# Weight tails as one DMA each, a buffer for every pair's exponentials, and a new order of all steps in a linear-attention and Mish block

## The chip, the cores and the metric

The kernel runs on one core of a Trainium2 chip. A core has five engines that run side by side and meet through semaphores: TensorE (PE in the profile; PEld is its weight load), VectorE (DVE), ScalarE (ACT), GpSimd (POOL) and SyncE (SP), which here only issues DMAs. The core's 16 DMA engines carry the transfers. The metric is the device time of one execution in microseconds (us); the profile gives one execution with the start and duration of each instruction, and of each DMA packet.

## What is computed

x has 2048 rows of 448 columns. All is bfloat16. Cut to what matters:

```python
xn = (x - mean(x)) / sqrt(var(x) + 1e-5)
q, k, v = split_heads(xn @ wqkv)                  # 16 heads of 28
pq, pk = q @ w_phi[h], k @ w_phi[h]               # per head, 28 x 28
phi_q = concat(softmax(pq), softmax(-pq)); phi_k likewise
kv, z = phi_k^T v, sum over rows of phi_k         # per head
attn = (phi_q kv) / (phi_q z + 1e-6) @ wo
h = xn @ w1 + b1                                  # 448 -> 1792
ffn = (h * tanh(softplus(h))) @ w2                # Mish
out = x + attn + ffn
```

## The kernel before

The 2048 rows are 16 tiles t of 128, handled as eight pairs u. The 448 columns of a contraction are three chunks of 128 and a tail of 64. The two tiles of a pair keep their tails in the lower and the upper 64 partitions of one chunk, so that two products of 64 rows can run together on PE; the last 64 rows of each weight are for that reason loaded into both halves of the partitions (`load_tail`, L260 to L263, two DMAs of 64 rows each).

The program records every instruction in the order in which the steps of the string `ORDER` (L149 to L162) are called, one stream for each engine; `Program.resolve` (L91) then finds the semaphore waits from what each instruction reads and writes. So `ORDER`, written out, sets the order on every engine and on both DMA queues (SP's, and ACT's for the steps with the ending `a`). Each engine works strictly in its order: an instruction that waits holds all behind it. The steps:

- `lx0`, `lx1`, `lx2`, `lx4` load x (tiles 0-1, 2-3, 4-7, 8-15); `lqm` and `lqt`, `lkm` and `lkt`, `lvm` and `lvt`, `l1m` and `l1t` load the main part and the tail of the weights for queries, keys, values and W1; `lp` loads w_phi, `lb` b1, `l2` W2, `lo` Wo.
- `st`, `xn`: LayerNorm statistics of a pair (DVE, with two small ACT operations for the root) and the normalized rows (on DVE with the ending `d`, on POOL with `p`), in `NXN` buffers in turn. `xt`: transpose of a pair, by PE and a copy (`a`, `d`), or by a DMA transpose on SP (`m`).
- `wt`, `wm`: the weights for queries and keys are multiplied by w_phi on the chip. `w_tr` (L459) transposes them, eight 128-column pieces a half, `w_mm` (L474) multiplies by the block-diagonal `Wbd` into `Wpq` and `Wpk`.
- `v`, `k`, `q`, `f`: products of a pair, a group of 1024 rows q0 or q1, and of FFN1 column block fc. Each has a full part `F` (three chunks) and a half part `H` (the tail), both through `pair_part` (L364). Its two PSUM banks come from `take2` (L337), the pair of eight banks that has been untouched longest. The closing part calls the evacuation: a copy for values, exponentials on ACT for keys and queries, Mish on ACT for FFN1.
- `kn`: sums and reciprocals of a pair's exponentials (DVE) and their product (POOL, `phik`, L532). `kv`: 32 small products into one PSUM pair held from the first kv to `kvz`, which masks it into `KVZ`. `nd`: numerator and denominator of a tile and seven DVE operations. `ot`: DMA transpose of the result; `wo`, `g`: output projection and FFN2 into the same banks; `sto`, `stt`: stores.

Keys' exponentials, normalized keys and values have three buffers each, in turn over the eight pairs. Twelve products of zeros (`warm`) run on PE at the start.

Of the kernel before, what the change touches and what calls it, by code (L numbers as in the profile page):

```python
# [169 lines left out]
def _kernel(es, nc, A_x, A_wqkv, A_w_phi, A_wo, B_w1, B_b1, B_w2, out):  # L170
# [120 lines left out]
    op("POOL", lambda e: e.memset(ident[:], 0.0), w=[("ident",)])  # L291
    op("POOL", lambda e: e.memset(eps_col[:], float(LN_EPS)), w=[("eps",)])
    op("POOL", lambda e: e.affine_select(out=ident[:], in_=ident[:], compare_op=ALU.not_equal, fill=1.0,
                                         base=0, pattern=[[-1, P]], channel_multiplier=1),
       r=[("ident",)], w=[("ident",)])
    op("POOL", lambda e: e.memset(mask[:], 1.0), w=[("mask",)])
    op("POOL", lambda e: e.affine_select(out=mask[:], in_=mask[:], compare_op=ALU.is_ge, fill=0.0, base=0,
                                         channel_multiplier=1, pattern=[[-DH, 4]]),
       r=[("mask",)], w=[("mask",)])
    op("POOL", lambda e: e.affine_select(out=mask[:], in_=mask[:], compare_op=ALU.is_ge, fill=0.0, base=DH - 1,  # L300
                                         channel_multiplier=-1, pattern=[[DH, 4]]),
       r=[("mask",)], w=[("mask",)])
    for i in range(NPH):
        op("POOL", lambda e, i=i: e.memset(v_ext[i][:, :, :, DH:DH + 1], 1.0), w=[("v1", i)])
    op("POOL", lambda e: e.memset(Wbd[:], 0.0), w=[("Wbd0",)])

    op("POOL", lambda e: e.memset(mask2[:], 1.0), w=[("mask2",)])
    for r in range(2):
        lo, hi = HALF[r]
        op("POOL", lambda e, lo=lo, hi=hi: e.affine_select(  # L310
            out=mask2[lo:hi], in_=mask2[lo:hi], compare_op=ALU.is_ge, fill=0.0, base=0, channel_multiplier=1,
            pattern=[[-DH, 2]]), r=[("mask2",)], w=[("mask2",)])
        op("POOL", lambda e, lo=lo, hi=hi: e.affine_select(
            out=mask2[lo:hi], in_=mask2[lo:hi], compare_op=ALU.is_ge, fill=0.0, base=DH - 1, channel_multiplier=-1,
            pattern=[[DH, 2]]), r=[("mask2",)], w=[("mask2",)])
    op("POOL", lambda e: e.tensor_copy(ap_on(KVZ[:, 0, 0, 0, DH + 1:DH + 2], [[NDW, 2 * G], [DH + 2, 2]]),
                                       ap_on(mask2[:, 0:1], [[0, 2 * G], [1, 2]])), r=[("mask2",)], w=[("KVZ1",)])

    def warm(e):
        for n in range(NWARM):  # L320
            ins = e.matmul(bank(0)[:, :], zeros[:, 0:P], zeros[:, :], start=True, stop=True)
        return ins
    op("DVE", lambda e: e.memset(zeros.bitcast(mybir.dt.uint32), 0), w=[("zeros",)], tag="zeros")
    op("PE", warm, r=[("zeros",)], w=[pb(0)], tag="warm")


# [497 lines left out]
```

## Time and profile before

| what | us |
|---|---|
| median of three runs (161.26 to 162.41) | 161.29 |
| the profiled execution: its span | 160.7 |
| PE, first product of values begins (L376) | 14.18 |
| last PE products, begin 144.57 and 13.40 long: end | 157.97 |
| last store issued | 158.67 |
| POOL, last phik begins | 53.2 |
| DVE, first nd operation | 59.02 |

The span is the profiled execution's own time from its first to its last instruction; it was taken apart from the three timed runs. The page's second part cuts it into 40 slices of 4.0 us, a digit for each engine's busy share in tenths. A timeline line has start, busy time, engine, line, operation, output and inputs, sizes and count; in brackets is the idle time before it and what ended it. A DMA line has tensor, queue, number of issues, KB of each and the median time from issue to landing.

### The profile page before, as it was taken

Reading aid. Unit: us, or ns where it says so; the run is one execution under the profiler, and the core shown is the slowest. Engines: PE = TensorE matmul, PEld = TensorE weight load, DVE = VectorE, ACT = ScalarE, POOL = GpSimd, SP = SyncE. Lnnn points to the kernel's source line nnn. Section 1 sums busy time; section 2 is a strip of 40 time slices with the busy share of each in tenths; the row PEclk is TensorE's granted clock in tenths of the full one; section 3 lists DMA queues with packets and bytes.
Section 4 is the critical chain, followed back from the end, with each engine's and each line's share of the span. In section 5 each row is a group of like instructions: output and inputs, shape, how many; then the busy total and the mean of one; then the engine's idle time right before and its main releaser. Section 6 shows DMA issues by size and latency. Waiting matters only on the chain.

```text
span 160.7 us, 3100 instructions
## 1 busy us (share of the span) xinstructions
PE 152.4 (95%) x1300; PEld 74.5 (46%) x1300; DVE 100.9 (63%) x209; ACT 75.6 (47%) x91; POOL 45.5 (28%) x73
## 2 busy tenths in 40 slices
PE   6659999998999999999999999999999999999993
PEld 2346545453444544434444454454545554555551
DVE  1768799999968168910778589988928811311131
ACT  2355988895939949997668756300100000000000
POOL 6766699959989600000000000000000000000000
PEclk9996999999999999999999999999999999999999
DMA  5998948240498000200030203060070130000502
GB/s 146 284 354 129 183 76 324 40 81 2 70 329 259 8 0 4 57 0 0 4 57 0 57 4 57 0 61 0 2 168 8 23 91 0 0 33 0 225 4 86
DMA packets 21306, 12.96 MB, mean 81 GB/s; under 512 B 14892, under 2 KB 20524, under 8 KB 21292
## 3 DMA queue, kind: packets, MB, share of 16 engines
q1 hardware_dynamic: 20524, 12.39, 30.6%
q10 hardware_dynamic: 768, 0.37, 0.9%
q8 instruction: 10, 0.16, 0.4%
q14 instruction: 4, 0.03, 0.1%
HBM read 7.48 MB, written 1.84 MB: 58 GB/s over the span
## 4 chain that ended last, share of the span: by engine, by line
PE 82%; POOL 5%; DVE 5%; DMA 4%; SPq 2%; issue 1%
PE PS L376 41%; PE PS L692 27%; PE PS L707 7%; POOL phik L532 4%; DMA Wq<-in_A_wqkv_dram 4%; PE PS L623 3%; DVE xn L421 2%; PE PS L553 2%; PE PS L481 1%; DVE Sk L528 1%; POOL xn L416 1%; PE PS L468 1%; SPq L262 1%; DVE v_ext L435 1%; SPq L257 0%
## 5 line engine op out<-in xcount | busy, mean ns | idle before, releaser
L376 PE MATMUL PS<-xnT,W 128*128 128x512 bf16 (+1 forms) x224 | 45.9, 379 | 0.0
L692 PE MATMUL PS<-W,actT 128*128 128x448 bf16 x224 | 43.5, 353 | 0.0
L602 ACT ACTIVATE actT<-PS,b1T 128x1024 bf16<-128x1024 f32 x28 | 30.0, 1112 | 21.3 <-PE PS L376 21.3
L692 PEld LDWEIGHTS PS<-W,actT 128*128 128x128 bf16 x224 | 21.8, 98 | 20.9 <-issue 0.8
L376 PEld LDWEIGHTS PS<-xnT,W 128*128 128x128 bf16 (+1 forms) x224 | 17.5, 97 | 23.4 <-issue 4.9
L532 POOL TENSOR_TENSOR phik<-Ek,rSk 128x896 bf16<-128x896 bf16 x16 | 26.8, 1699 | 2.6 <-DVE rSk L530 2.5
L682 DVE TENSOR_TENSOR x_all<-PS,x_all 128x448 bf16<-128x448 f32 x16 | 9.8, 622 | 25.8 <-PE PS L692 24.6
L528 DVE TENSOR_REDUCE Sk<-Ek 128x32 f32<-128x896 bf16 x16 | 16.8, 1050 | 0.6 <-ACT Ek L518 0.6
L588 ACT ACTIVATE EqT<-PS 128x1024 bf16<-128x1024 f32 x16 | 15.2, 1030 | 0.4 <-PE PS L376 0.2
L518 ACT ACTIVATE Ek<-PS 128x896 bf16<-128x896 f32 x16 | 13.8, 915 | 3.3 <-PE PS L376 3.2
L376 PE MATMUL PS<-xnT,Wpq 128*128 128x512 bf16 (+1 forms) x64 | 13.9, 379 | 0.7 <-DVE v_ext L435 0.7
L639 DVE COPY Sq<-PS 128x16 f32<-128x16 f32 x32 | 4.0, 168 | 16.7 <-PE PS L623 16.5
L376 PE MATMUL PS<-Wpk,xnT 128*128 128x448 bf16 (+1 forms) x64 | 13.0, 356 | 0.0
L376 PE MATMUL PS<-Wv,xnT 128*128 128x448 bf16 (+1 forms) x64 | 12.9, 360 | 0.0
L416 POOL TENSOR_SCALAR xn<-x_all,rstd,shift 128x448 bf16<-128x448 bf16 (+2 forms) x21 | 12.1, 589 | 0.7
L395 DVE BATCH_NORM_STATS2 stats<-x_all 128x6 f32<-128x448 bf16 x16 | 9.5, 596 | 3.3 <-DMA x_all<-in_A_x_dram 3.3
L647 DVE TENSOR_TENSOR Ek<-Ek,phik 128x464 f32<-128x464 f32 x16 | 10.3, 642 | 0.6
L643 DVE TENSOR_TENSOR Ek<-PS,Sq 128x464 f32<-128x464 f32 x16 | 10.3, 642 | 0.5
L650 DVE TENSOR_TENSOR xn<-Ek,rden 128x448 bf16<-128x448 f32 x16 | 10.0, 625 | 0.6
L645 DVE TENSOR_TENSOR phik<-PS,Sq 128x464 f32<-128x464 f32 x16 | 10.1, 631 | 0.0
L376 PEld LDWEIGHTS PS<-xnT,Wpq 128*128 128x128 bf16 (+1 forms) x64 | 5.2, 97 | 7.0 <-DVE v_ext L435 1.1
L376 PEld LDWEIGHTS PS<-Wpk,xnT 128*128 128x128 bf16 (+1 forms) x64 | 5.1, 97 | 6.3 <-issue 2.1
...
## 6 DMA issues: line engine op xcount, KB each, us to landing
...
out_dram<-x_all SPq DMA_DIRECT2D x7, 224.0 KB, 2.1
W<-in_B_w_dram SPq DMA_DIRECT2D x1, 1344.0 KB, 6.2
...
Wo<-in_A_wo_dram SPq DMA_DIRECT2D x2, 336.0 KB, 9.3
...
W<-in_B_w_dram SPq DMA_DIRECT2D x2, 224.0 KB, 4.1
Wk<-in_A_wqkv_dram SPq DMA_DIRECT2D x1, 336.0 KB, 4.4
```

Of the source, the lines that this page charges most:

```text
L376: ins = e.matmul(o, lhs(c, k), rhs(c, k), start=first and c in (0, 3), stop=not first and c in (2, 3))
L416: op("POOL", lambda e, t=t, lo=lo, hi=hi, at=at: e.tensor_scalar(X[:, at:at + hi - lo], x_all[:, t, lo:hi], rstd[:, t:t + 1], shift[:, t:t ...
L518: op("ACT", lambda e, s=s: e.activation(Ek[i][:, s, :, :], two(b, D), ACT.Exp, scale=1.0 if s == 0 else -1.0), r=[pb(b), pb(b + 1)], w=[(" ...
L528: op("DVE", lambda e: e.tensor_reduce(Sk[i][:, s, :], Eh(), AX.X, ALU.add), r=[("Ek", i, s)], w=[("Sk", i, s)], tag=f"Sk{u}.{s}")
L532: op("POOL", lambda e: e.tensor_tensor(phik[j][:, s, :, :].rearrange("p i (h f) -> p (i h) f", f=DH), Eh(), ap_on(rSk[i][:, s, 0:1], [[1, ...
L588: op("ACT", lambda e, s=s: e.activation(EqT[:, s, g, q * 1024:(q + 1) * 1024], bank(b, 2), ACT.Exp, scale=1.0 if s == 0 else -1.0), r=[pb( ...
L602: op("ACT", lambda e: e.activation(actT[:, fc, q * 1024:(q + 1) * 1024], bank(b, 2), ACT.Mish, bias=b1T[:, fc:fc + 1]), r=[("b1T",), pb(b) ...
L643: op("DVE", lambda e: e.tensor_tensor(tv(t1[i]), num(0), sx(1), ALU.mult), r=[pb(b), pb(b + 1), ("Sq", i, 1)], w=[("t1", i)], tag=f"ta{t}")
L645: op("DVE", lambda e: e.tensor_tensor(tv(t2), num(1), sx(0), ALU.mult), r=[pb(b), pb(b + 1), ("Sq", i, 0)], w=[("t2",)], tag=f"tb{t}")
L647: op("DVE", lambda e: e.tensor_tensor(t1[i], t1[i], t2, ALU.add), r=[("t1", i), ("t2",)], w=[("t1", i)], tag=f"tc{t}")
L692: ins = e.matmul(bank(b)[:, 0:D], actT[:, fc, tok(t)], W2[:, fc, :], start=first and fc == 0, stop=last and fc == FC - 1)
L707: ins = e.matmul(bank(b)[:, 0:D], oT_of(u)[lo:hi, cc * P:(cc + 1) * P], Wo[lo:hi, cc, :], start=first and c in (0, 3), stop=last and c in ...
```

## The change

- Each tail is one DMA into all 128 partitions, whose source goes over the 64 rows twice by an outer step of zero. Keys' and values' weights lie in one tensor `Wkv` and share one tail of 64 rows by 896 columns. All loads are on SP's queue, in the order x1, x0, Wk, key/value tail, w_phi, b1, Wv, x2, x4, query tail, Wq; then transposes of pairs 2, 7, 6, 3, Wo, pair 4, W1 tail, pair 5, W1, W2.
- All eight pairs have their own exponentials, in columns of `actT` that FFN1 (blocks 6 to 13) fills later; they are normalized in place. Values of all pairs lie in one tensor, sums have eight buffers, xn four, and `WT` one per weight and half.
- The root of LayerNorm is a step of its own (`rs`), for seven pairs on POOL as an addition and a power of -0.5. Seven of eight pairs are normalized on DVE (one before); x1 and x0 are transposed on PE, the other six by DMA (one and seven before).
- The setup instructions of POOL, DVE and PE are steps of the order too. Values come ahead of keys, the pairs in the order 0, 1, 2, 7, 6, 3, 4, 5, and all kv steps after them, among the first FFN1 steps.

The diff, cut; what is left out is the setup as functions with the same instructions, and renamed operands.

```diff
--- before.py
+++ after.py
...
@@ -147,18 +146,18 @@
 
 
 ORDER = """
-lx1s lpa lx0a lqta lkts bd lkms lbs lx2s table st1 st0 b1 wtk1d wtk0a lqms xn1p lvts lvms wmk1a xn0p st2 lx4s
-wtq1d xt1d xn2p wmk0a wmq1a st3 wtq0d v1Hd k1H k1F xt0m st4 v1Fd wmq0a xn3p xn4p xt2m k0F v0Ha l1ts k0H k2H
-kn1.0 st7 xt3m kn1.1 v0Fa v2Fa v2Ha kn0.1 q0.2H k2F q0.2F kn0.0 xt4m v4Fd st5 xn5p k3F kn2.1 kv1 v4Hd k3H k4F
-kv0 k4H kn2.0 xn7d q0.0H q0.1H q0.1F kn3.0 l1ms xt5m q0.0F kn4.1 v3Fd k5F st6 kv2 v3Hd v5Ha xn6p k5H kn4.0 v5Fa
-q0.3F xt7m k7H xt6m q0.3H k7F v7Fd kv4 kn3.1 kv3 kn5.1 v6Ha kn5.0 v7Hd v6Fa k6F k6H q1.0H kn7.0 q1.2H kn7.1
-q1.0F q1.2F f1.3F l2s kn6.1 f0.7F f1.3H f0.7H kv5 kn6.0 kv7 kv6 f0.1F kvz f0.3F nd2 f1.2H f0.3H f0.1H f1.2F
-q1.1F nd3 q1.1H nd1 los q1.3H q1.3F f0.4H f0.4F f0.8F f0.2F f0.5F f0.8H f0.2H f0.5H f1.1H f1.1F f1.4F f0.0F
-f1.4H ot1m f0.0H f1.13H nd0 f1.13F f1.5F f1.7F f1.7H f1.6H nd7 f1.6F f1.10F ot0m f1.10H nd6 ot3m f1.5H f0.10H
-f0.10F f1.0F nd5 f1.0H f0.6H f0.11H f0.6F f0.11F f1.12F nd4 f1.11H f1.12H nd10 f1.11F f0.13F f0.12F f0.12H ot2m
-f0.13H nd8 f0.9H f0.9F f1.8F nd11 nd9 f1.8H wo0H g1 g0 wo0F ot5m wo3F nd14 wo3H nd15 ot7m f1.9H f1.9F g6 g7 g11
-ot4m wo5H wo2H nd12 nd13 wo5F g5 wo4F wo2F sto3 g10 ot6m g4 g15 wo7H wo6H wo1H sto0 wo4H g8 wo7F wo6F g13 wo1F
-stt15 g9 sto4 g12 g2 sto5 sto6 g3 sto2 sto1 g14 stt14
+pm table lx1s zero pk st1 lx0s lkms pv pw lkts pi lps rs1p z12 st0 lbs xn1d rs0a bd xn0d lvms wtk0a wtk1d lx2s b1
+xt1a xt0d wmk0a st2 wmk1a v0Fd rs2p lx4s v1Fa xn2d lqts k0H st7 v1Ha k1H v0Ha lqms xt2m k0F rs7p xn7d st6 k1F rs6p
+wtq0d wtq1d v2Hd k2H k2F v2Fa xt7m xn6d st3 wmq1a k7F rs3p wmq0a v7Fd v7Ha k7H xt6m k6H xn3d v6Ha xt3m kn2.0 st5 rs5p
+k6F st4 rs4p v6Fd xn4p los xn5d xt4m l1ts q0.2F kn6.0 k3H q0.2H xt5m q0.0H v3Hd kn0.0 k3F kn1.1 l1ms kn0.1 q0.0F
+q0.3F kn2.1 v3Fa k4F q0.3H k4H q0.1H kn7.0 v4Hd v4Fd q0.1F kn3.0 k5F v5Fd v5Hd l2s k5H q1.0H q1.3H kn5.0 q1.3F kn4.0
+kn7.1 kn6.1 q1.0F q1.2F kn3.1 f1.1F q1.2H f1.4H f1.1H f1.4F kn5.1 f0.1F kv7 kv2 kv6 kv0 f0.1H f0.3H q1.1H q1.1F f0.0F
+f0.3F kn4.1 kn1.0 kv4 kv1 kv3 kv5 f0.5F kvz f0.0H f0.8H f0.5H nd1 f0.8F f1.11F f0.4F f1.11H nd2 f0.4H f0.6F f0.6H nd3
+f0.11H f0.9H f0.11F f0.9F f0.10F f1.2H f0.10H ot1m nd0 f0.13H f1.2F f1.9F f0.13F f1.7F f1.7H nd6 f1.9H ot0m f1.12H
+f1.12F f0.12F nd4 f0.12H f1.6H nd5 f1.6F f0.2H f0.2F f0.7F ot2m f0.7H f1.3H nd7 f1.8H ot3m f1.8F f1.3F f1.0F f1.10F
+nd8 f1.10H f1.5H f1.0H f1.5F g1 wo0H nd10 f1.13H nd9 f1.13F g0 wo0F wo1F g3 ot4m nd12 nd13 wo1H wo3H g6 ot6m wo3F
+wo4F g7 g2 g9 nd11 sto1 ot5m wo4H nd15 nd14 g8 wo6F g12 g5 wo5F sto0 g13 ot7m g11 wo7F wo6H sto4 sto6 wo5H wo2H wo7H
+sto3 g14 g10 wo2F g4 g15 sto5 sto2 stt14 stt15
 """
 
...
+    eps_col = sb("eps_col", [P, 1], FP32)
+    mhalf = sb("mhalf", [P, 2], FP32)
...
-    NXN = 3
+    NXN = 4
...
-    Wv = sb("Wv", [P, 4, D], BF16)
-    Wqk = [sb("Wq", [P, 4, D], BF16), sb("Wk", [P, 4, D], BF16)]
+    Wkv = sb("Wkv", [P, 4, 2 * D], BF16)
+    Wk, Wv = Wkv[:, :, 0:D], Wkv[:, :, D:2 * D]
+    Wq = sb("Wq", [P, 4, D], BF16)
+    Wqk = [Wq, Wk]
...
-    WT = [sb(f"WT{i}", [GP, 2, G, P], BF16) for i in range(2)]
+    WT = [[sb(f"WT{w}{i}", [GP, 2, G, P], BF16) for i in range(2)] for w in range(2)]
...
-    NE = 3
-    Ek = [sb(f"Ek{i}", [P, 2, 2, D], BF16) for i in range(NE)]
-    Sk = [sb(f"Sk{i}", [P, 2, 2 * H], FP32) for i in range(NE)]
-    rSk = [sb(f"rSk{i}", [P, 2, 2 * H], FP32) for i in range(NE)]
-    NPH = 3
-    phik = [sb(f"phik{i}", [P, 2, 2, D], BF16) for i in range(NPH)]
-    v_ext = [sb(f"v_ext{i}", [P, 2, H, DH + 1], BF16) for i in range(NPH)]
+    Sk = [sb(f"Sk{i}", [P, 2, 2 * H], FP32) for i in range(NU)]
+    rSk = [sb(f"rSk{i}", [P, 2, 2 * H], FP32) for i in range(NU)]
+    v_flat = sb("v_all", [P, NU * 2 * H * (DH + 1)], BF16)
+    v_all = v_flat[:, :].rearrange("p (u i h c) -> p u i h c", u=NU, i=2, h=H)
...
+    def as_t(n):
+        return v_flat[:, :].bitcast(FP32)[:, n * H * (DH + 1):(n + 1) * H * (DH + 1)].rearrange("p (h c) -> p h c", c=DH + 1)
+
+    t1, t2 = [as_t(0), as_t(1)], as_t(2)
+
+    FE = FC - NU
+
+    def E_of(u):
+        return actT[:, FE + u, 0:4 * D].rearrange("p (s i d) -> p s i d", s=2, i=2)
+
+    oT_home = [(Wkv, 0, ["Wk", "Wv"]), (Wkv, 14 * P, []), (Wq, 0, ["Wq"]), (Wp[1], 0, ["Wp1"])]
+    home_rows = {"Wk": [("Wk", 0), ("Wt",)], "Wv": [("Wv", 0)], "Wq": [("Wq", i) for i in range(2)],
+                 "Wp1": [("Wp", 1, h) for h in range(2)]}
...
     def load_tail(eng, name, dst, src):
-        for i, (lo, hi) in enumerate(HALF):
-            dma(eng, lambda e, lo=lo, hi=hi: e.dma_start(dst[lo:hi, 3, :], src[384:448, :]), w=[(name, 1 + i)],
-                tag="ld" + name)
+        dma(eng, lambda e: e.dma_start(dst[:, 3, :], bass.AP(
+            tensor=src.tensor, offset=src[384:448, :].offset, ap=[[0, 2]] + [list(d) for d in src[384:448, :].ap])),
+            w=[("Wt",) if name == "Wkv" else (name, 1)], tag="ld" + name)
 
     def rows_of(name):
-        return [(name, i) for i in range(3)]
+        return [(name, 0), ("Wt",)] if name in ("Wk", "Wv") else [(name, i) for i in range(2)]
...
+    def p_ident():
+        op("POOL", lambda e: e.memset(mhalf[:], -0.5), w=[("mhalf",)], tag="mhalf")
+        op("POOL", lambda e: e.memset(eps_col[:], float(LN_EPS)), r=[("mhalf",)], w=[("eps",)], tag="eps")
+        op("POOL", lambda e: e.memset(ident[:], 0.0), w=[("ident",)], tag="pi0")
...
+    def ln_rstd(u, eng):
         a, b = 2 * u, 2 * u + 2
+        if eng == "POOL":
+            op("POOL", lambda e: e.tensor_scalar(lnv[:, a:b], mv[:, a:b, 1], float(LN_EPS), 0.0, op0=ALU.add,
+                                                 op1=ALU.add),
+               r=[("mv", a), ("mv", a + 1)], w=[("lnv", u)], tag=f"vare{u}")
+            op("POOL", lambda e: e.tensor_tensor(rstd[:, a:b], lnv[:, a:b], mhalf[:], ALU.pow),
+               r=[("lnv", u), ("eps",)], w=[("rstd", u)], tag=f"rstd{u}")
+            return
         op("ACT", lambda e: e.activation(lnv[:, a:b], mv[:, a:b, 1], ACT.Ln, bias=eps_col[:]),
            r=[("eps",), ("table",), ("mv", a), ("mv", a + 1)], w=[("lnv", u)], tag=f"ln{u}")
...
         if eng == "POOL":
-            op("POOL", lambda e: e.tensor_tensor(shift[:, a:b], mv[:, a:b, 0], rstd[:, a:b], ALU.mult),
+            op("DVE", lambda e: e.scalar_tensor_tensor(shift[:, a:b], mv[:, a:b, 0], -1.0, rstd[:, a:b], ALU.mult,
+                                                       ALU.mult),
                r=[("mv", a), ("mv", a + 1), ("rstd", u)], w=[("sh", u)], tag=f"sh{u}")
-            op("POOL", lambda e: e.tensor_scalar(shift[:, a:b], shift[:, a:b], -1.0, 0.0, op0=ALU.mult, op1=ALU.add),
-               r=[("sh", u)], w=[("sh", u)], tag=f"sj{u}")
...
-        pe(tr, rows_of("Wq" if which == 0 else "Wk") + [("ident",)], [pb(b)], f"wtr{which}{h}")
-        evac(eng, lambda: WT[h][:, :, :, :].rearrange("p c g n -> p (c g n)"),
-             lambda: oT().rearrange("p c g n -> p (c g n)"), [pb(b)], [("WT", h)], f"wtre{which}{h}")
+        pe(tr, rows_of("Wq" if which == 0 else "Wk")[:1 + 2 * h] + [("ident",)], [pb(b)], f"wtr{which}{h}")
+        evac(eng, lambda: WT[which][h][:, :, :, :].rearrange("p c g n -> p (c g n)"),
+             lambda: oT().rearrange("p c g n -> p (c g n)"), [pb(b)], [("WT", which, h)], f"wtre{which}{h}")
...
     def k_mm(u, part):
-        i = u % NE
-
         def then(b):
             for s in range(2):
-                op("ACT", lambda e, s=s: e.activation(Ek[i][:, s, :, :], two(b, D), ACT.Exp,
+                op("ACT", lambda e, s=s: e.activation(E_of(u)[:, s, :, :], two(b, D), ACT.Exp,
                                                       scale=1.0 if s == 0 else -1.0),
-                   r=[pb(b), pb(b + 1)], w=[("Ek", i, s)], tag=f"exk{u}.{s}")
+                   r=[pb(b), pb(b + 1)], w=[("E", u, s)], tag=f"exk{u}.{s}")
         pair_part(f"k{u}", part, tok_works(u, Wp[1]), [("xnT", u)] + [("Wp", 1, h) for h in range(2)], then)
 
     def k_norm(u, s):
-        i, j = u % NE, u % NPH
-
         def Eh():
-            return Ek[i][:, s, :, :].rearrange("p i (h f) -> p (i h) f", f=DH)
-        op("DVE", lambda e: e.tensor_reduce(Sk[i][:, s, :], Eh(), AX.X, ALU.add), r=[("Ek", i, s)], w=[("Sk", i, s)],
+            return E_of(u)[:, s, :, :].rearrange("p i (h f) -> p (i h) f", f=DH)
+        op("DVE", lambda e: e.tensor_reduce(Sk[u][:, s, :], Eh(), AX.X, ALU.add), r=[("E", u, s)], w=[("Sk", u, s)],
            tag=f"Sk{u}.{s}")
-        op("DVE", lambda e: e.reciprocal(rSk[i][:, s, :], Sk[i][:, s, :]), r=[("Sk", i, s)], w=[("rSk", i, s)],
+        op("DVE", lambda e: e.reciprocal(rSk[u][:, s, :], Sk[u][:, s, :]), r=[("Sk", u, s)], w=[("rSk", u, s)],
            tag=f"rSk{u}.{s}")
-        op("POOL", lambda e: e.tensor_tensor(phik[j][:, s, :, :].rearrange("p i (h f) -> p (i h) f", f=DH), Eh(),
-                                             ap_on(rSk[i][:, s, 0:1], [[1, 2 * H], [0, DH]]), ALU.mult),
-           r=[("Ek", i, s), ("rSk", i, s)], w=[("phik", j, s)], tag=f"phik{u}.{s}")
+        op("POOL", lambda e: e.tensor_tensor(Eh(), Eh(), ap_on(rSk[u][:, s, 0:1], [[1, 2 * H], [0, DH]]), ALU.mult),
+           r=[("E", u, s), ("rSk", u, s)], w=[("E", u, s)], tag=f"phik{u}.{s}")
...
-        pe(f, [("phik", j, 0), ("phik", j, 1), ("v", j), ("v1", j)], [pb(kvb)], f"kv{u}")
+        pe(f, [("E", u, 0), ("E", u, 1), ("v", u), ("v1",)], [pb(kvb)], f"kv{u}")
...
-               r=[("b1T",), pb(b), pb(b + 1)], w=[("act", fc, q)], tag=f"mish{q}_{fc}")
+               r=[("b1T",), pb(b), pb(b + 1)],
+               w=[("act", fc, q)] + ([("E", fc - FE, s) for s in range(2)] if fc >= FE else []), tag=f"mish{q}_{fc}")
...
-        for i, n in enumerate("qkv"):
-            args = eng, "W" + n, (Wqk + [Wv])[i], A_wqkv[:, i * D:(i + 1) * D]
-            add(f"l{n}m{c}", load_main, *args)
-            add(f"l{n}t{c}", load_tail, *args)
+        for i, (n, t) in enumerate((("q", Wq), ("k", Wk), ("v", Wv))):
+            add(f"l{n}m{c}", load_main, eng, "W" + n, t, A_wqkv[:, i * D:(i + 1) * D])
+        add(f"lqt{c}", load_tail, eng, "Wq", Wq, A_wqkv[:, 0:D])
+        add(f"lkt{c}", load_tail, eng, "Wkv", Wkv, A_wqkv[:, D:3 * D])
         add(f"l1m{c}", load_main, eng, "W1", W1, B_w1)
         add(f"l1t{c}", load_tail, eng, "W1", W1, B_w1)
```

More of the change, by code (lines that the diff above doesn't have):

```diff
@@ L26 @@
 DEN_EPS = 1e-6
-NWARM = 12
 QP = 56
@@ L287, in table @@
            tag="table")
[L291 to L324, printed above, removed]
+    def p_ident():
+        op("POOL", lambda e: e.memset(mhalf[:], -0.5), w=[("mhalf",)], tag="mhalf")
+        op("POOL", lambda e: e.memset(eps_col[:], float(LN_EPS)), r=[("mhalf",)], w=[("eps",)], tag="eps")
+        op("POOL", lambda e: e.memset(ident[:], 0.0), w=[("ident",)], tag="pi0")
+        op("POOL", lambda e: e.affine_select(out=ident[:], in_=ident[:], compare_op=ALU.not_equal, fill=1.0,
+                                             base=0, pattern=[[-1, P]], channel_multiplier=1),
+           r=[("ident",)], w=[("ident",)], tag="pi1")
@@ new lines, in p_mask @@
+    def p_mask():
+        op("POOL", lambda e: e.memset(mask[:], 1.0), w=[("mask",)], tag="pm0")
+        op("POOL", lambda e: e.affine_select(out=mask[:], in_=mask[:], compare_op=ALU.is_ge, fill=0.0, base=0,
+                                             channel_multiplier=1, pattern=[[-DH, 4]]),
+           r=[("mask",)], w=[("mask",)], tag="pm1")
+        op("POOL", lambda e: e.affine_select(out=mask[:], in_=mask[:], compare_op=ALU.is_ge, fill=0.0, base=DH - 1,
+                                             channel_multiplier=-1, pattern=[[DH, 4]]),
+           r=[("mask",)], w=[("mask",)], tag="pm2")
@@ new lines, in p_wbd, with p_ones, p_mask2 @@
+    def p_wbd():
+        op("POOL", lambda e: e.memset(Wbd[:], 0.0), w=[("Wbd0",)], tag="pw0")
+    def p_ones():
+        op("POOL", lambda e: e.memset(v_all[:, :, :, :, DH:DH + 1], 1.0), w=[("v1",)], tag="pv0")
+    def p_mask2():
+        op("POOL", lambda e: e.memset(mask2[:], 1.0), w=[("mask2",)], tag="pk0")
+        for r in range(2):
+            lo, hi = HALF[r]
+            op("POOL", lambda e, lo=lo, hi=hi: e.affine_select(
+                out=mask2[lo:hi], in_=mask2[lo:hi], compare_op=ALU.is_ge, fill=0.0, base=0, channel_multiplier=1,
+                pattern=[[-DH, 2]]), r=[("mask2",)], w=[("mask2",)], tag="pk1")
+            op("POOL", lambda e, lo=lo, hi=hi: e.affine_select(
+                out=mask2[lo:hi], in_=mask2[lo:hi], compare_op=ALU.is_ge, fill=0.0, base=DH - 1, channel_multiplier=-1,
+                pattern=[[DH, 2]]), r=[("mask2",)], w=[("mask2",)], tag="pk2")
+        op("POOL", lambda e: e.tensor_copy(ap_on(KVZ[:, 0, 0, 0, DH + 1:DH + 2], [[NDW, 2 * G], [DH + 2, 2]]),
+                                           ap_on(mask2[:, 0:1], [[0, 2 * G], [1, 2]])), r=[("mask2",)], w=[("KVZ1",)],
+           tag="pk3")
@@ L328, in _kernel, with zero, warm, f @@
+    def zero():
+        op("DVE", lambda e: e.memset(zeros.bitcast(mybir.dt.uint32), 0), w=[("zeros",)], tag="zeros")
+    def warm(n):
+        b = take1()
+        def f(e):
+            for _ in range(n):
+                ins = e.matmul(bank(b)[:, :], zeros[:, 0:P], zeros[:, :], start=True, stop=True)
+            return ins
+        pe(f, [("zeros",)], [pb(b)], f"warm{n}")
     clock = [0]
@@ L725, in _kernel @@
         add(f"st{u}", ln_stats, u)
+        for eng, c in (("ACT", "a"), ("POOL", "p")):
+            add(f"rs{u}{c}", ln_rstd, u, eng)
         for eng, c in (("DVE", "d"), ("POOL", "p")):
```

33 lines of the change are left out of this document (14 added, 19 removed).

## The prediction

> **What bounds the kernel now.** I read the page's busy shares and slices first, then TensorE's (PE's) own order of time, its waits, the table by stage and the DMA issues.
>
> ```profile
> PE 152.4 (95%) x1300; PEld 74.5 (46%) x1300; DVE 100.9 (63%) x209; ACT 75.6 (47%) x91; POOL 45.5 (28%) x73
> ...
> PE   6659999998999999999999999999999999999993
> ...
> PEclk9996999999999999999999999999999999999999
> ```
>
> PE is full from the fourth slice (4.0 us each) to the last, so time can be won only in the first three slices, and lost by any new hole.
>
> ```profile
> 1.25 4.34 PE L321 MATMUL PS<-actT 128*128 128x512 bf16 x12 [1.25 <-DVE actT L323]
> 7.03 0.18 PE L596 MATMUL PS<-ident,b_rows 14*128 14x14 bf16 x1 [1.43 <-DMA b_rows<-in_B_b_dram]
> 7.13 1.10 PE L468 MATMUL PS<-ident,Wk 128*112 128x128 bf16 x16
> 8.66 0.55 PE L481 MATMUL PS<-Wbd,WT 112*128 112x112 bf16 x8 [0.43 <-DVE WT L435]
> 10.58 0.65 PE L468 MATMUL PS<-ident,Wq 128*112 128x128 bf16 x8 [1.36 <-DMA Wq<-in_A_wqkv_dram]
> ...
> 13.19 1.06 PE L468 MATMUL PS<-ident,Wq 128*112 128x128 bf16 x8
> 14.18 0.55 PE L376 MATMUL PS<-Wv,xnT 64*128 64x448 bf16 x2
> ```
>
> The columns are start, busy time, line, operands, count. From 14.18 PE streams values, keys, queries and the rest until 157.97. Ahead of that it waits for loads.
>
> ```profile
> PE PS L376 <- DVE v_ext L435: 0.7, 1, 0.7
> ...
> PE PS L553 <- POOL phik L532: 0.4, 1, 0.4
> ```
>
> These two, 1.1 us, are the only holes after 14.18.
>
> ```profile
> 8.00:12.00 4.00, 2.21 (x33) 1.93 (x31) 2.75 (x7) 2.40 (x4) 2.63 (x8) 0.91 1.07 355
> 12.00:16.00 4.00, 4.00 (x32) 2.78 (x31) 3.58 (x9) 2.32 (x5) 2.52 (x7) 0.66 0.81 128
> ...
> 24.00:28.00 4.00, 4.00 (x51) 2.12 (x51) 3.86 (x8) 3.71 (x6) 3.85 (x4) 1.00 0.85 327
> ```
>
> The last three columns are granted clock, DMA share and GB/s. The DMA engines are full in the head: one engine moves 355/(1.07x16) = 21 GB/s there and 327/(0.85x16) = 24 with W1's long rows. And a hole costs twice: 0.09x4 + 0.34x4 = 1.7 us of clock went after PE's idling from 7.9 to 10.6.
>
> ```profile
> W<-in_B_w_dram SPq DMA_DIRECT2D x1, 1344.0 KB, 6.2
> ...
> W<-in_B_w_dram SPq DMA_DIRECT2D x2, 224.0 KB, 4.1
> Wk<-in_A_wqkv_dram SPq DMA_DIRECT2D x1, 336.0 KB, 4.4
> ...
> b_rows<-in_B_b_dram SPq DMA_DIRECT2D x1, 3.5 KB
> ```
>
> Of b_rows two things are to be seen. It has 3.5 KB, was issued at 3.28, and PE got it at 7.03: it stood behind Wk (landed 6.90) in each DMA engine's line, so loads of a queue go in order. And it alone has no landing time. The trace's semaphore record shows why: loads whose outer dimension is 128, 112 or 64 give 16 arrivals; b_rows, 14 rows, gives one at 3.98 and fourteen between 5.96 and 6.98. It was dealt to 14 engines, one row each, with the missing two signed off at once.
>
> **The change part by part.** The sum is against the profiled span of 160.7 us; the median of the runs shown is 161.29, so 0.6 is added at the end.
>
> *Tails as single loads.* The old tail is two loads of 64 rows. The new one reads the 64 rows twice, with an outermost source dimension of 2 (step 0). If the outer dimension deals out the work, as for b_rows, two engines carry each tail, 64 rows each, and what stands behind it in the queue waits on those two. The trace leaves open whether the source's 2 or the destination's 128 partitions counts; I take 2, since b_rows shows that an outer dimension below 16 is not cut further.
>
> The Trainium skill, "DMA: Bandwidth & Descriptors", section "Why a DMA increments its semaphore by 16 and not by 1", says that the number of engines is the largest one up to 16 that divides the outer dimension of both sides. By that rule it is 2 here and the sum is the one below; for 14 rows the trace agrees with it (14 late arrivals).
>
> Packet times, means of the trace's packet records: 896 bytes 49 ns, 1792 bytes 78 (x, 2 rows), 3584 bytes 154 (148 for W1), 7168 bytes 297, 256 bytes of a transpose 28. On the two engines, in the new queue order: x1 and x0 8x78 = 0.62 each, Wk 24x49 = 1.18, key/value tail 64x78 = 5.0, w_phi 0.3, Wv 1.18, x2 1.23, x4 2.38, query tail 64x49 = 3.1, Wq 1.18. Before, the sum up to Wk was 3.5, first packet at 2.0, landed 6.9: 1.4 around it. So Wk lands at 2.0+2.4+1.4 = 5.8, its tail at 10.8, w_phi and b1 11.1, Wv 12.3, x2 13.5, x4 15.9, Wq 20.2.
>
> *The head.* PE transposes Wk's first half at 5.8 to 6.6, then waits for the tail until 10.8; behind that in its order stand the bias, both x transposes and the products for Wpk. The clock is then half from 11.3 as before (the same slices idle): 0.9 for the second half (0.99 at 13.19 before), 0.1, two x transposes 14x107 ns = 1.5, products 1.6 (16 at 11.59 took that). Values start at 14.9. ScalarE's (ACT's) copy of the first half, VectorE's (DVE's) xT0 copy (by 14.0) and Wv lie under it.
>
> Left for PE: before, 157.97-14.18 = 143.8, less 1.1 of holes and 0.35 of half clock, is 142.4. Query preparation now comes later: 16 transposes and 8 products, 0.9+0.45. Changes between full and half height fall from 65 to 62, 0.1 each. So 143.4, and an end at 158.3: 0.3 later than before.
>
> *The W1 tail* (3584-byte rows). It is issued right after the transpose of pair 4 and ahead of that of pair 5. PE: values and keys of pairs 0, 1, 2, 7, 6 at 1.4 each and query preparation, 15.8, plus 0.2 for pair 2's transpose: done 30.9. Then DVE's v6 copy 1.1, the shift 0.2, GpSimd's (POOL's) xn4 1.73, the issue of pair 4's transpose 1.22: the tail is issued at 35.3. W1's main load took 6.25 from issue (22.14) to landing, 24 packets of 148 ns an engine, 3.55, and 2.7 around them. The tail takes 64x148 = 9.5, pair 5's transpose behind it 56x28 = 1.6: it lands at 35.3+2.7+9.5+1.6 = 49.1. PE comes to k5 after four query groups (1.6 each, means of the trace from start to start), two of keys (1.45) and two of values (1.4), 12.1: at 43.0. It waits 6.1 us, and nothing in its order can pass; behind it are v5, q1 and all of FFN1, and POOL's last eight normalizations through kn5.0. The clock then costs 1.7 again (0 if PE came back within a slice; I take the row's).
>
> *Own buffers for exponentials, values in one tensor, WT per weight, 4 xn buffers.* They take away waits only: at most the 1.1 us of holes, which I have taken out. The first FFN1 columns that overwrite exponentials follow the last kv.
>
> *LayerNorm roots on POOL by a power.* Seven pairs of small ACT operations (0.5 each) leave ACT, which idles there anyway. A power has no row: from 0.19 (POOL's 128x2 product) to 1.7 (its largest product); nearest in shape 0.2. Three stand on DVE's chain, so +4.5 at the top end. DVE takes 7 of 8 xn (before 1): alone 0.4 a piece (the one of 384 columns took 0.37), beside POOL's products up to 1.67; POOL is idle where six of them stand, the seventh runs beside xn4 (up to +1.5 on POOL's start, whose chain has 0.7 to spare at kv1).
>
> *ACT's loads moved to SP.* Four DMAs, 2 us of ACT issue, now behind x1 on SP: priced in the queue above. SP issues seven loads by 4.7, ahead of their data. Each transpose waits on SP for its xn; loads queued behind it (Wo 4.3 us of issue, W1, W2) are needed later than they come: by the same packet sums W1's main part lands near 53 and W2 near 58; FFN1 begins near 58, and FFN2 after 100.
>
> *Setup as steps, late order.* POOL builds the masks first, so the identity comes at about 4.8 (the same instructions end at 4.3 before, and a longer memset of ones, 0.5 to 0.75 as its nearest two rows, is among them); Wk's landing at 5.8 hides it, with 1.0 to spare. The gaps between nd steps hold DVE's 3.0 us chain and the 3 us transposes, as before; the last steps end alike: 2.75 from PE's end to the span's end.
>
> Sum: 158.3+6.1+1.7+2.75 = 168.9, with 0.6: **169.4 us**.
>
> **Rivals.**
> 1. *Sixteen engines* (the destination's 128 partitions decide). The tail then costs 0.62 and lands at 6.4, Wv 7.9, x2 9.1. DVE: statistics of x1 and x0 3.7 to 6.8, xn1 7.6, xn0 8.4; PE transposes until 8.9, products until 9.9, values at 9.9, no half clock. 9.9+143.4+1.1 (holes as before)+2.75+0.6 = 157.7, faster. For it: each load of the trace into 128 partitions went to 16 engines. Against: b_rows. It decides from five engines on: 9.5x(1-2/5) = 5.7 is taken off k5's wait.
> 2. *Two engines, but pair 5's transpose is not held* (it passes the tail, or PE is later at k5 than worked out). Only the head counts: 158.3+2.75+0.6 = 161.6. For it: the other transposes land 3 us after issue. Against: b_rows behind Wk.
> 3. *Two engines and a slow power or a late POOL*: 1.5 to 3 on top, 171.5. No row speaks for it.
>
> **How the numbers follow.** Two engines with the hole at k5: 0.64; rival 1: 0.17; rival 2: 0.13; rival 3: 0.06. About 1% is what a measurement of this kernel can tell from no change. Faster 0.17 (rival 1), within 1% 0.12 (rival 2, nearly all), slower 0.71. The likeliest case has its own range of 166 to 172: 2 us for the wait, 1.7 for the clock. The range runs from rival 2's 161.0 to 172.5, with rival 1 left out.
>
> **What would show it.** The key/value, query and W1 tails: their landing times, about 8, 13 and 12 us after issue, or 4 to 7 if rival 1 holds. PE's hole ahead of the second Wk transposes, 6.6 to 10.8, and the hole at k5 near 43, named after the xnT transpose. A clock digit of 5 to 7 in the slices near 12 and near 49. Values start near 14.9 (rival 1: 9.9). The prediction is wrong if the tails land with 16 engines' speed, or if FFN1 starts before 50 us.

## The result and the profile after

| | us | ratio to before, 95% interval |
|---|---|---|
| before, median of 4 runs (161.26 to 162.41) | 161.55 | |
| after, median of 4 runs (174.05 to 175.77) | 174.82 | 1.082 (1.076 to 1.087) |
| after, the profiled execution; its span | 174.56; 172.6 | |

The change costs 8.2%. From the profile's page after, the busy times and two rows of slices (now 4.3 us each):

```profile
PE 155.7 (90%) x1307; PEld 76.2 (44%) x1307; DVE 102.1 (59%) x227; ACT 74.3 (43%) x79; POOL 39.8 (23%) x54
...
PE   7539999899208999999999999999999999999993
...
PEclk9956999999955899999999999999999999999999
```

PE's busy time grew by 3.3 us, about what the longer stretches at half clock add to it, and its share fell from 95% to 90%: it has new holes. There are two, in the third slice and in the eleventh and twelfth, and the granted clock falls in both places. PE's order of time gives them (start, busy time, line, operands, count, and in brackets the idle time before and what ended it):

```profile
6.64 0.62 PE L493 MATMUL PS<-ident,Wkv 128*112 128x128 bf16 x8 [0.41 <-DMA Wkv<-in_A_wqkv_dram]
11.43 1.10 PE L493 MATMUL PS<-ident,Wkv 128*112 128x128 bf16 x8 [4.17 <-DMA Wkv<-in_A_wqkv_dram]
12.46 0.19 PE L613 MATMUL PS<-ident,b_rows 14*128 14x14 bf16 x1
12.59 1.67 PE L453 MATMUL PS<-ident,xn 128*128 128x128 bf16 x14
14.05 1.70 PE L506 MATMUL PS<-Wbd,WT 112*128 112x112 bf16 x16
```

```profile
42.90 1.46 PE L393 MATMUL PS<-xnT,Wpq 128*128 128x512 bf16 x6
52.21 2.40 PE L393 MATMUL PS<-Wpk,xnT 128*128 128x448 bf16 x6 [7.86 <-DMA xnT<-xn]
54.40 2.82 PE L393 MATMUL PS<-Wkv,xnT 128*128 128x448 bf16 x8
57.05 0.35 PE L393 MATMUL PS<-Wpk,xnT 64*128 64x448 bf16 x2
57.24 4.58 PE L393 MATMUL PS<-xnT,Wpq 64*128 64x512 bf16 x22
61.67 0.59 PE L393 MATMUL PS<-xnT,W 128*128 128x512 bf16 x2
```

The first hole is the second half of Wk's transposes, waiting for the key/value tail; values follow at 15.54. The second is pair 5's keys, waiting for pair 5's transpose. The table by stage has the clock in the third column from the right, then the DMA share and GB/s:

```profile
8.00:12.00 4.00, 0.57 (x5) 0.57 (x6) 0.03 (x1) 0.32 (x1) 0.33 (x1) 0.65 1.01 296
12.00:16.00 4.00, 4.00 (x38) 3.62 (x38) 2.44 (x6) 1.88 (x3) 0.75 (x2) 0.50 0.34 118
...
40.00:60.00 20.00, 12.14 (x56) 4.67 (x55) 8.51 (x13) 8.36 (x10) 8.76 (x7) 0.74 1.03 181
```

SP's queue shows where the second hole comes from (start, time of the issue):

```profile
36.56 1.24 SPq L465 DMA_TRANSPOSE xnT<-xn  x1
37.84 0.57 SPq L264 DMA_DIRECT2D W<-in_B_w_dram  x1
38.46 5.98 SPq L465 DMA_TRANSPOSE xnT<-xn  x1
44.48 1.04 SPq L260 DMA_DIRECT2D W<-in_B_w_dram  x1
```

Pair 4's transpose leaves in 1.24. W1's tail follows, and the issue of pair 5's transpose behind it takes 5.98. The landings, from the semaphore record: W1's tail at 49.74, 11.9 after its issue, and pair 5's transpose at 52.07, 13.6 after its own (the other five took 2.9 to 3.1). The DMA list has the same in another form:

```profile
W<-in_B_w_dram SPq DMA_DIRECT2D x1, 448.0 KB
...
Wkv<-in_A_wqkv_dram SPq DMA_DIRECT2D x1, 224.0 KB
```

No landing time stands behind them, as with b_rows before: a tail gives three arrivals on its semaphore and not 16. The key/value tail's came at 3.25, 11.35 and 11.39. Two engines carried it.

### The profile page after: what moved, and what is told of

Same layout as the page of the kernel before. It is cut to its first block, busy times and chain, and to the rows that moved or that the text cites. A ratio compares the mean times of both kernels' runs of the same rounds, so it can differ in the third digit from the quotient of the medians.

```text
span 172.6 us, 3081 instructions
## 1 busy us (share of the span) xinstructions
PE 155.7 (90%) x1307; PEld 76.2 (44%) x1307; DVE 102.1 (59%) x227; ACT 74.3 (43%) x79; POOL 39.8 (23%) x54
## 4 chain that ended last, share of the span: by engine, by line
PE 70%; DMA 13%; DVE 11%; POOL 2%; issue 1%; SPq 1%; DVEq 0%
PE PS L393 33%; PE PS L710 25%; DMA xnT<-xn 8%; PE PS L725 6%; DMA Wkv<-in_A_wqkv_dram 5%; DVE stats L412 4%; DVE xn L446 3%; PE PS L641 2%; PE PS L570 2%; DVE Sk L547 2%; POOL rstd L422 2%; DVE mv L414 1%; PE PS L453 1%; DVE WT L460 1%; PE PS L493 1%
## 5 line engine op out<-in xcount | busy, mean ns | idle before, releaser
L551 POOL TENSOR_TENSOR actT<-actT,rSk 128x896 bf16<-128x896 bf16 x16 | 26.6, 1697 | 14.2 <-DVE rSk L549 14.2
L393 PE MATMUL PS<-Wpk,xnT 128*128 128x448 bf16 (+1 forms) x64 | 14.0, 373 | 7.9 <-DMA xnT<-xn 7.9
L700 DVE TENSOR_TENSOR x_all<-PS,x_all 128x448 bf16<-128x448 f32 x16 | 9.6, 620 | 18.7 <-PE PS L710 10.8
L539 ACT ACTIVATE actT<-PS 128x896 bf16<-128x896 f32 x16 | 13.6, 930 | 11.1 <-PE PS L393 11.1
L547 DVE TENSOR_REDUCE Sk<-actT 128x32 f32<-128x896 bf16 x16 | 16.6, 1040 | 0.0
L393 PE MATMUL PS<-Wkv,xnT 128*128 128x448 bf16 (+1 forms) x64 | 14.4, 381 | 0.0
L393 PE MATMUL PS<-xnT,Wpq 128*128 128x512 bf16 (+1 forms) x64 | 13.8, 380 | 0.4 <-ACT actT L539 0.4
L665 DVE TENSOR_TENSOR v_all<-v_all 128x464 f32<-128x464 f32 x16 | 10.3, 642 | 0.6
L661 DVE TENSOR_TENSOR v_all<-PS,Sq 128x464 f32<-128x464 f32 x16 | 10.3, 642 | 0.5
L668 DVE TENSOR_TENSOR xn<-v_all,rden 128x448 bf16<-128x448 f32 x16 | 10.0, 625 | 0.7
L663 DVE TENSOR_TENSOR v_all<-PS,Sq 128x464 f32<-128x464 f32 x16 | 10.1, 630 | 0.0
L460 DVE CAST v_all<-PS 128x896 bf16<-128x896 f32 x3 | 3.2, 1061 | 11.3 <-PE PS L393 11.3
L393 PEld LDWEIGHTS PS<-Wkv,xnT 128*128 128x128 bf16 (+1 forms) x64 | 5.8, 104 | 7.2 <-issue 3.1
## 6 DMA issues: line engine op xcount, KB each, us to landing
W<-in_B_w_dram SPq DMA_DIRECT2D x1, 1568.0 KB, 14.4
```

The source lines that it names most:

```text
L393: ins = e.matmul(o, lhs(c, k), rhs(c, k), start=first and c in (0, 3), stop=not first and c in (2, 3))
L539: op("ACT", lambda e, s=s: e.activation(E_of(u)[:, s, :, :], two(b, D), ACT.Exp, scale=1.0 if s == 0 else -1.0), r=[pb(b), pb(b + 1)], w=[ ...
L547: op("DVE", lambda e: e.tensor_reduce(Sk[u][:, s, :], Eh(), AX.X, ALU.add), r=[("E", u, s)], w=[("Sk", u, s)], tag=f"Sk{u}.{s}")
L551: op("POOL", lambda e: e.tensor_tensor(Eh(), Eh(), ap_on(rSk[u][:, s, 0:1], [[1, 2 * H], [0, DH]]), ALU.mult), r=[("E", u, s), ("rSk", u, ...
L661: op("DVE", lambda e: e.tensor_tensor(tv(t1[i]), num(0), sx(1), ALU.mult), r=[pb(b), pb(b + 1), ("Sq", i, 1)], w=[("t1", i)], tag=f"ta{t}")
L663: op("DVE", lambda e: e.tensor_tensor(tv(t2), num(1), sx(0), ALU.mult), r=[pb(b), pb(b + 1), ("Sq", i, 0)], w=[("t2",)], tag=f"tb{t}")
```

## The experiments

**Halves for all tails.** Everything as changed, but each tail is again two loads of 64 rows.

```diff
-        dma(eng, lambda e: e.dma_start(dst[:, 3, :], bass.AP(
-            tensor=src.tensor, offset=src[384:448, :].offset, ap=[[0, 2]] + [list(d) for d in src[384:448, :].ap])),
+        for i, (lo, hi) in enumerate(HALF):
+            dma(eng, lambda e, lo=lo, hi=hi: e.dma_start(dst[lo:hi, 3, :], src[384:448, :]), ...
```

> The changed kernel, with every tail as two loads of 64 rows again (the key/value tail as two of 64 rows by 896 columns); all else as changed. Theory (each single tail is carried by two DMA engines, and what stands behind it in the queue waits): the tails land about 4 us after issue, values begin near 10.3 us in place of 15.5, the hole ahead of k5 (7.9 us and 2.4 us of half clock) is gone: 174.8 - 5.2 - 10.3 = 159.3 us, a little under the kernel before. Rival (the new order, the power on POOL or the late kv steps are at fault): 172 to 175 us, holes stay.

Measured: 160.44 us, 0.991 of before (0.988 to 0.994). All of the 13 us lost came back with this one edit, and a little more. PE's order of time in the head of this run, and at pair 5's keys:

```profile
7.97 0.65 PE L512 MATMUL PS<-ident,Wkv 128*112 128x128 bf16 x8 [0.24 <-DMA Wkv<-in_A_wqkv_dram]
8.56 0.18 PE L632 MATMUL PS<-ident,b_rows 14*128 14x14 bf16 x1
8.67 0.95 PE L472 MATMUL PS<-ident,xn 128*128 128x128 bf16 x14
9.46 0.95 PE L525 MATMUL PS<-Wbd,WT 112*128 112x112 bf16 x16
10.34 1.88 PE L412 MATMUL PS<-Wkv,xnT 128*128 128x448 bf16 x9
...
40.63 1.29 PE L412 MATMUL PS<-Wpk,xnT 128*128 128x448 bf16 x6 [0.42 <-DMA xnT<-xn]
41.76 1.59 PE L412 MATMUL PS<-Wkv,xnT 128*128 128x448 bf16 x8
```

Values start 5.2 us earlier. The 14 x transposes take 0.95 and not 1.67, the six key products 1.29 and not 2.40, because the clock stays at full (granted 1.00 in this run from 8 to 20 and from 40 to 60 us). This version also takes 0.9% less than the kernel before (interval 0.6 to 1.2%): that is what the rest of the change is worth. It is less than the head gains (values at 14.18 before): from there to its last product PE now takes 145.6 us against 143.8, where the preparation of the query weights, 1.35 by the prediction's count, now lies behind the start of the values.

**Halves for W1 alone, halves for the head alone.** The same edit for one group of tails each.

> The changed kernel with W1's tail alone as two loads of 64 rows. Theory: the head is unchanged (values at 15.5), the hole at k5 and the half clock after it are gone: 174.8 - 10.3 = 164.5 us. Rival (it is the place of W1's tail ahead of pair 5's transpose that counts, whatever engines carry it): the hole stays and the time is within 2 us of 174.8.

> The changed kernel with the key/value and query tails as two loads of 64 rows each, W1's tail single. Theory: values begin near 10.3 us; W1's tail is issued as much earlier as PE is, so the hole at k5 stays about 8 us with its half clock: 174.8 - 5.2 = 169.6 us. If the two places were one delay seen twice, the time would be near 159 like the kernel with all tails split.

Measured: with W1's tail in halves 165.03 us, ratio 1.020 (1.015 to 1.024); with the key/value and query tails in halves 170.26, ratio 1.051 (1.044 to 1.058). The first keeps the head's hole (4.7) and has 0.3 at pair 5's keys; the second starts values at 9.79 and has the other hole whole:

```profile
47.27 2.40 PE L412 MATMUL PS<-Wpk,xnT 128*128 128x448 bf16 x6 [8.01 <-DMA xnT<-xn]
```

So the head's tails cost 174.82-170.26 = 4.6 and W1's tail 174.82-165.03 = 9.8. Together that is 14.4, and both at once gave 174.82-160.44 = 14.4: within the intervals, about 1 us each way, the losses add. Starting 5.7 us earlier did not shorten the wait at pair 5, since W1's tail moves with the rest (issued at 32.73, landed at 44.79).

**What deals a load out: the outer dimension, or the rows read twice?** Two loads of 64 rows per tail, with sources that name every row once, but nested: an outer dimension of `n` = 2, or of 16. The rows of the tail come in another order, so both kernels compute something else.

```diff
+                part = bass.AP(tensor=src.tensor, offset=rows.offset,
+                               ap=[[step, n], [step * n, 64 // n], list(cols)])
```

> Every weight tail is again two loads of 64 rows, as in the version of 160.4 us, but the source of each is written with an outer dimension of 2 and a step that is not zero (rows 0, 2, 4, ... and then 1, 3, 5, ...). The rows of the tail therefore lie in another order, and the output is not that of the reference. Theory (the outer dimension of the source is what deals a load out, here to two engines): the key and value tail lands after 11 us, the values start after 15 us, pair 5's transpose again waits behind W1's tail and PE stands 6 to 9 us at its keys; 172 to 176 us. If the two loads fall on different pairs of engines, half of that: 165 to 168. Rival (the step of zero, the same rows read twice, is what costs): 160 to 161 us, values at about 10.3.

> The same as the kernel with an outer dimension of 2, with 16 in its place (again the rows of the tails lie in another order and the output is not the reference's). Both theories expect the time of plain halves, 160 to 161 us with the values at about 10.3; anything near 174 would say that neither the number 2 nor the step of zero is the cause, but the nested form of the source itself.

Measured: 175.75 us for 2 (ratio 1.089, 1.084 to 1.094) and 159.99 for 16 (0.990, 0.987 to 0.994). The DMA lists of the two, first 2, then 16:

```profile
W<-in_B_w_dram SPq DMA_DIRECT2D x2, 224.0 KB
...
Wkv<-in_A_wqkv_dram SPq DMA_DIRECT2D x2, 112.0 KB
```

```profile
W<-in_B_w_dram SPq DMA_DIRECT2D x2, 224.0 KB, 4.7
...
Wkv<-in_A_wqkv_dram SPq DMA_DIRECT2D x2, 112.0 KB, 4.3
```

The same bytes from the same rows: three arrivals a load and no landing time with an outer 2, sixteen and 4.3 to 4.7 us with an outer 16. The step of zero is innocent; the number 2 is the cause. The two halves of the key/value tail with an outer 2 landed at 8.99 and 12.39, one behind the other, so both fell on the same two engines. The Trainium skill, "DMA: Bandwidth & Descriptors", section "Why a DMA increments its semaphore by 16 and not by 1", counts the engines as the largest number up to 16 that divides the outer dimensions of both sides; these two runs agree with it (2 and 16).

**The single tails in the old order.** The kernel before, with nothing changed but `load_tail`.

> The kernel before with nothing changed but the weight tails, each now a single load whose source has the outer dimension of 2. Theory (the single tails alone are the loss): its head puts the query and the key tails first, so Wk's rows wait behind 64 packets of each on two engines: the head comes 5 to 6 us later, and W1's tail, issued among the transposes, holds the next pair by 5 to 7 more, with 1 to 2 us of half clock: 172 to 176 us. Rival (the tails cost only in the new order, where every load is on one queue): 162 to 164 us.

Measured: 174.53 us, ratio 1.080 (1.074 to 1.086), 0.3 from the whole change. PE's order of time in this run:

```profile
11.17 0.19 PE L596 MATMUL PS<-ident,b_rows 14*128 14x14 bf16 x1 [4.62 <-DMA b_rows<-in_B_b_dram]
...
32.79 0.61 PE L376 MATMUL PS<-xnT,Wpq 64*128 64x512 bf16 x2 [6.79 <-DMA xnT<-xn]
```

The same two holes, at other places: Wk's rows landed at 10.95 behind two tails, and W1's tail (issued at 19.31, landed at 31.71) held the next pair's transpose, issued at 22.49, until 32.65.

**W1's tail behind pair 5's transpose.**

```diff
-... xt4m l1ts q0.2F kn6.0 k3H q0.2H xt5m q0.0H ...
+... xt4m q0.2F kn6.0 k3H q0.2H xt5m l1ts q0.0H ...
```

> The changed kernel with one step moved: the single load of W1's tail is issued right after the transpose of pair 5 in place of ahead of it. Theory (in order on each engine): the hole at k5 is gone; W1's main part, behind the tail, lands near 55 us, while PE would come to FFN1 at about 51.5, so a wait of 3 to 4 us with some half clock takes its place: 174.8 - 10.3 + 4.5 = 169 us. Rival (the tail slows the transposes by load on the DMA engines, not by its place in the queue): the hole at k5 stays, 173 to 176 us.

Measured: 173.92 us, ratio 1.076 (1.072 to 1.080), and I had it 5 us too low. The wait at pair 5 is gone, and FFN1 waits in its place, for 6.87 us where I had 3 to 4:

```profile
41.00 1.30 PE L393 MATMUL PS<-Wpk,xnT 128*128 128x448 bf16 x6 [0.15 <-DMA xnT<-xn]
...
59.80 2.72 PE L393 MATMUL PS<-xnT,W 128*128 128x512 bf16 x6 [6.87 <-DMA W<-in_B_w_dram]
```

The tail took 15.8 us (40.48 to 56.31), not 12, as W1's main rows and W2's were issued right behind it and packets of 3584 bytes took 219 ns in the mean, against 152 in the changed kernel. W1's main part itself landed at 59.71, 18.6 after its issue. In this run the head's hole was also 0.8 us longer, and PE waited 1.3 for pair 2's transpose. Here, moving the slow load only moved the loss to the large loads behind it.

**W1's tail on ACT's queue.**

```diff
-... xt4m l1ts q0.2F ...
+... xt4m l1ta q0.2F ...
```

> The changed kernel with W1's single tail issued from ACT's queue instead of SP's, at the same place in the list of steps. Theory (pair 5's transpose waits because it is behind the tail in SP's queue, and SP itself is held by the two full engines): SP issues pair 5's transpose and W1's rows at once, the transpose shares the two engines with the tail and lands by 45 to 46 instead of 52.1, PE's wait at its keys is 0 to 2 us, and the time is 166 to 169 us. Rival (an engine serves what it was handed first, from whichever queue): the transpose still lands at 49 to 52 and the time is 173 to 175. The head, with its wait of 4.2 and its half clock, is the same in both.

Measured: 172.32 us, ratio 1.070 (1.062 to 1.077): neither theory's number. ACT did not wait for pair 4's rows as SP did, so the tail left 5.2 us earlier (32.61) and landed at 45.35. Pair 4's transpose was issued at 37.93 by SP and landed at 45.93, pair 5's at 46.82: both right behind the tail, though they came from another queue. PE now waits for pair 4:

```profile
46.06 2.32 PE L393 MATMUL PS<-Wpk,xnT 128*128 128x448 bf16 x6 [5.14 <-DMA xnT<-xn]
```

So it is not SP's queue alone that holds a transpose. But the tail does not shut out the other queue either. Wo's last two loads, issued by SP at 32.77 and 33.34 with sixteen arrivals each, landed at 38.68 and 39.50, ahead of the tail. And of pair 4's transpose some 300 packets of 256 bytes began between 41.8 and 44.7, while the tail's packets still ran; in the changed kernel, with both on one queue, no packet of pair 5's transpose began in the tail's last 8.7 us. From the other queue a transfer is slowed by the tail; why both transposes still landed only behind it stays open.

**The price of the power.** First, all roots on ACT, each issued behind its statistics; then the power replaced by a product (which leaves the rows unnormalized).

```diff
-xt1a xt0d wmk0a st2 wmk1a v0Fd rs2p ...
+xt1a xt0d wmk0a st2 rs2a wmk1a v0Fd ...
```

```diff
-op("POOL", lambda e: e.tensor_tensor(rstd[:, a:b], lnv[:, a:b], mhalf[:], ALU.pow),
+op("POOL", lambda e: e.tensor_tensor(rstd[:, a:b], lnv[:, a:b], mhalf[:], ALU.mult),
```

> The changed kernel with its single tails, but all the reciprocal roots on ACT (logarithm and exponential, 0.3 and 0.2 us each) in place of POOL (0.2 and 0.7), each issued right behind its statistics. Theory (the power on POOL, 0.5 us dearer than I took it, made W1's tail leave 2.5 us late): the tail is issued at about 35.5 instead of 37.8, pair 5's transpose lands at about 49.7 instead of 52.1, PE's wait at pair 5's keys falls from 7.9 to 5.5, and the time is 172 to 173 us. Rival (the roots lie beside other work, and something else made the tail late): the wait stays 7.5 to 8 and the time within 0.5 us of 174.8.

> The changed kernel with the power on POOL replaced by a product on the same tiles, so the rows are not normalised to unit variance and the output is not the reference's. It prices the power by itself. Theory (0.7 us for the power, of which three stand on DVE's chain ahead of W1's tail): the product takes 0.2, each of DVE's waits of 1.1 us for a root shrinks by 0.5, W1's tail is issued at 36.0 to 36.5 instead of 37.8, PE's wait at pair 5's keys falls from 7.9 to 6.2 to 6.6, and the time is 173.0 to 173.5 us. Rival (DVE catches up before W1's tail): the tail leaves at 37.5 or later and the time stays within 0.5 us of 174.8.

Measured: 174.91 us with the roots on ACT (ratio 1.084, 1.078 to 1.091), no gain; 172.75 with the product (1.071, 1.065 to 1.076). DVE's waits for the root, in the changed kernel, with ACT, and with the product (total, times, longest):

```profile
DVE xn L446 <- POOL rstd L422: 3.4, 3, 1.1
```

```profile
DVE xn L446 <- ACT rstd L427: 3.3, 3, 2.1
```

```profile
DVE xn L446 <- POOL rstd L422: 1.9, 3, 0.6
```

On ACT the roots stand behind exponentials in ACT's order, and DVE waits as long as before (the tail left at 38.34); that run says nothing on the power. The product does. POOL's line in the changed kernel and with the product (busy time, mean ns, idle time before):

```profile
L422 POOL TENSOR_TENSOR rstd<-lnv,mhalf 128x2 f32<-128x2 f32 x7 | 4.9, 703 | 0.6
```

```profile
L422 POOL TENSOR_TENSOR rstd<-lnv,mhalf 128x2 f32<-128x2 f32 x7 | 1.4, 197 | 0.6
```

The instruction falls from 703 to 197 ns, W1's tail leaves at 36.40 instead of 37.84, PE's wait falls from 7.86 to 6.88, and the time by 2.1 us (1.8 by the ratios). The power is worth that.

**Halves, and the roots on ACT.**

> All tails in two loads and all roots on ACT. Theory (what is left of PE's waits for normalised rows, 1.4 us in three places, hangs on POOL's roots): 159.0 to 159.6 us. Rival (ACT's 0.5 us a pair delays the values' copies and the exponentials, which hold PE's banks): 160.4 to 161.5 us.

Measured: 160.96 us, ratio 0.997 (0.994 to 1.000), so the rival's case, not a gain: PE's waits for normalized rows fell from 1.4 to 0.4, but it waited 1.5 for ACT's copy of Wpk and 0.9 for the exponentials.

## Why the prediction was right in kind and short in size

The forecast was the likeliest case's mechanism, 169.4 us, within 161.0 to 172.5. The time is 174.82, beyond the upper end. Two engines a tail, the two holes and the half clock behind them came where they were forecast. Two terms of the sum failed: when W1's tail is issued, 2.5 us too early because the power was taken at 0.2 us and measured 0.70, and the time outside the span, 1.35 too small. The terms beside what the profiled execution shows:

| term | worked out | measured |
|---|---|---|
| values start | 14.9 | 15.54 |
| W1's tail issued | 35.3 | 37.84 |
| from there until pair 5's transpose has landed | 13.8 | 14.2 |
| PE comes to pair 5's keys | 43.0 | 44.35 |
| its wait there | 6.1 | 7.86 |
| half clock behind it | 1.7 | 2.4 |
| from PE's return to the span's end | 119.8 | 120.4 |
| span | 168.9 | 172.6 |
| outside the span | 0.6 | 1.95 |

- *Two engines a tail*: right. Wk's tail landed at 11.39 (10.8), Wv at 12.5 (12.3), x2 at 13.63 (13.5), x4 at 15.85 (15.9), Wq at 19.39 (20.2). The outer 2 against 16 shows the cause.
- *The head*: right within 0.64. The hole came where I put it, and the clock stayed at half until 16.02.
- *The issue of W1's tail, the step that failed*. "A power has no row": between 0.19 and 1.7 I took 0.2, "nearest in shape". It took 0.70, on top of an addition of 0.22. I took the row that was like it in shape, and an operation of another kind was the point. The tail left 2.5 us late; of that the head's delay is 0.64 and the run with the product gives 1.44 for the power. The other 0.5 I did not trace (the terms that I listed add up to 35.15, not 35.3). I had the bound ("+4.5 at the top end") in the text and not in the range's upper end, where it belonged; by itself it would have put that end at 173.9, still short.
- *Pair 5's transpose behind it*: right. The tail's packets took 142 ns in the mean between 42 and 48 us, 11.9 us in all (12.2 worked out). The 148 taken came near by luck: W1's main packets before took 166 in the mean and 140 in the median. The transpose behind it took 2.3, not 1.6.
- *The half clock*: 0.7 short. I took the head's row, where PE had worked between two waits of 0.43 and 1.36, so not after one hole of 2.7; behind 7.86 it lasted until 56.98, 4.8 us at half.
- *Outside the span, the other failed term*: I set the span of one execution beside the median of several. In all executions that list both, the kernel before has 1.68 to 1.81 outside its span, the changed one 1.87 to 2.08. So the profiled execution before took about 162.4, which fits the slowest of the three times and is hardly one apart from them, and my 0.6 was 1.7 outside the span less the 1.1 by which it lay above the median. The changed kernel's profiled execution lies 0.26 below its median. This makes 1.35 of the miss.
- *Own buffers, values first, setup as steps*: the two waits before, 1.1 us, are gone, as I took out; one of 0.44 for an exponential is new. The memset of ones took 1.21, not 0.5 to 0.75, and Wk's landing hid it. DVE's rows took 0.89 a pair, where I had 0.4 a piece.

The power also moved the path to the tail. In the sum PE's values of pair 6 release DVE's copy, and the tail follows from there. PE was done with them at 31.62, but DVE reached the copy only at 33.12, with no idle time ahead of it: DVE's own chain of statistics, root and rows set the pace, with three waits of 1.1 us for POOL. With the product in place of the power, DVE waits for PE there, as in the sum. The copy in the changed kernel, and with the product:

```profile
33.12 1.06 DVE L460 CAST v_all<-PS 128x896 bf16<-128x896 f32 x1
```

```profile
31.97 1.09 DVE L460 CAST v_all<-PS 128x896 bf16<-128x896 f32 x1 [0.19 <-PE PS L393]
```

The sum: 3.1 us for PE's later return, 0.6 behind it, 1.35 outside the span, and 0.3 between the profiled run and the median: 5.3, and 0.1 of rounding. Rival 1, sixteen engines, is what the halves show: 160.44 where I had 157.7, the time outside the span (1.3) and the head (0.4) among the difference; most of the rest is PE's stretch from the first values to its last product, 145.6 against 144.5. Rival 2 is excluded by the waits of 7.86 and 8.01 at pair 5. Rival 3, two engines and a slow power, is what the runs show: it put 1.5 to 3 on top, and the run with the product gives 2.1. I gave it a chance of 0.06, since no row spoke for it; none spoke against it either, and its 171.5 was nearer than 169.4. The range's lower end of 161.0 is called rival 2's, whose sum is 161.6.
